# One product over both chunks for the levels of 16 and 32 steps of the first tile

## The chip, the cores and the metric

The program runs on one core of one Trainium2 chip. The metric is the device time of one execution in microseconds (us). Before the change it is 591.69 us, the median of three executions (591.05 to 592.04).

The core's engines work side by side, each through its own list of instructions in order, and wait for one another through semaphores. PE multiplies matrices, and PEld names its loads of weights; DVE, ACT and POOL work on elements; SP starts most DMA transfers. A matmul takes its weights (`lhsT`, a block of rows by columns) and streams the columns of `rhs` past them, and its result goes to PSUM.

## The reference

There are two blocks, one behind the other. The first is a recurrent attention (RWKV-6): for each of 4 batches and 8 heads, over 768 steps of 48 channels, a 48 x 48 state is kept.

```python
for t in range(S):
    cur = einsum('bhd,bhe->bhde', u * k[t], v[t])
    y[t] = einsum('bhd,bhde->bhe', r[t], state + cur)
    state = w[t][..., None] * state + einsum('bhd,bhe->bhde', k[t], v[t])
```

The second takes y, laid out as 3072 tokens of 384 channels, and computes `gelu(x @ w_in) @ w_out` with the exact gelu, 2048 hidden channels and an output of 3072 x 384. `w_in` and `w_out` come as 64-bit numbers and are turned into 32-bit ones on the chip. All matmuls on data are in 32-bit floats.

## The kernel before, in words

**Tiles and units.** The sequence is cut into 8 tiles x = 0 to 7 of T = 384 steps (two for each batch), and a tile into 6 chunks of C = 64 steps. Two heads share the 128 partitions, 64 rows each (48 used), so 8 heads are 4 pairs. Tile 0 alone is worked in two units of two pairs each (`units_of(0)` is 2, so `np_` is 1 there and 2 in later tiles), so that its work can start before all of its data is there. NI = 6 is the number of (pair, double chunk) entries in a unit.

**Inside a chunk.** For step t and an earlier step s of the same chunk, r of t meets k of s through the product of the decays w between them. Tiles 0 and 1 build this 64 x 64 matrix `a_sb` by levels of h = 1, 2, 4, 8, 16 and 32 steps (`halves`). At level h the chunk falls into blocks of 2h steps, and the later half of every block meets its earlier half. A level has three parts:

- `products` (L480): for each entry, each head g and each of its two chunks p, a matmul with the chunk's k as 64 rows x 64 columns of weights and the chunk's r as 64 moving columns. Results of the two chunks go to rows 0 to 63 and 64 to 127 of the PSUM pair `d`, those of the two heads to its two banks. In tile 0 all 64 columns of r are multiplied and the later halves are picked out of the result by a view; later tiles multiply only the 32 columns of the later halves.
- the update (L522, L533): DVE multiplies r and k by decays, in place, for the next level. It can start when the product has read them.
- the copy to `a_sb`: below level 16 by DVE with a mask (L544), at levels 16 and 32 by ACT, one copy (L541) for each block, 4 a unit at level 16 and 2 at level 32.

In tile 0 every `products` call except the one of level 1 ends with `keep_warm(2)` (L253), two matmuls of zeros, 128 x 512 in bf16, whose result nobody reads. The pool of `d` has three pairs of banks, so a product waits for the copies out of the pair used three before.

**After the levels.** PE transposes k (L713, `kt_ps`), ACT copies the result to SBUF (L715, `kx`), PE multiplies k and v of each chunk (L739, `kv_ps`), DVE runs the chain of states over the chunks (L759, L754), and PE multiplies `a_sb` with v (L780) and r with the states (L825) into `y_ps`. ACT and DVE copy y to `xT` (L832, L848), and one pair of heads goes by way of `ysb` (ACT, L851) and six small DMAs (L855, three issued by SP and three by ACT).

**The order of work.** It is written out by hand: each stage is a generator, and the string `PLAN[x]` says whose next step comes. For tile 0, "." and "s" are the two units, "f" the start of tile 1's attention, "c" the conversion of the weights (three ACT passes L361, L362, L364, two DVE passes L373, L377), "l" the loads, "w" the load of tile 1's v, "x" six more matmuls of zeros. Every engine gets its instructions in this order, so the conversions stand between the attention's steps on ACT and DVE. The memsets of L232 and L191 on DVE release loads that SP issues (L233, L192).

**After tile 0.** Tile 1's attention runs beside the projections of tile 0: L1216 makes the hidden rows `h_ps`, ACT applies gelu (L1219, L1221), L1310 and later L1230 multiply with `w_out`. L1004 is the projection in the later tiles.

## Time and profile before

| what | value |
|---|---|
| median of three executions | 591.69 us |
| the profiled execution | 593.44 us, span 591.6 us |
| PE busy, loads of weights busy | 572.6 us (97%), 509.1 us (86%) |
| DVE, ACT busy | 461.9 us (78%), 276.6 us (47%) |
| PE busy from 0 to 10 us | 4.48 us |
| PE busy from 30 to 40 us | 6.39 us |
| PE busy from 50 to 60 us | 10.00 us |
| one product of levels 4 to 32 in tile 0 (L480) | 0.93 us, 48 records of matmuls and 48 of loads |
| a pair of `keep_warm` matmuls there | 0.39 us |
| the 12 copies of levels 16 and 32 (L541) | 4.50 us, from 29.83 us on |
| the first L1216 | at 47.47 us |

The profile shows one execution. A row of the timeline gives the start, the length, engine, line and operation of some instructions of one kind that follow each other, how many (x), and in brackets how long the engine had been idle before them and what ended that. A matmul in 32-bit floats stands in the profile as two records, with two loads of weights. Lengths of single matmuls overlap, so the time of a group is its length as a whole. "Issue" as a cause means that nothing in the profile accounts for the wait.

### The profile page before, as it was taken

To read this page: it belongs to the slowest core of one execution; us is meant where nothing else is said; L and a number is where in the kernel's file an instruction comes from. 1 tells how busy PE (TensorE), PEld (TensorE's weight loads), DVE (VectorE), ACT (ScalarE), POOL (GpSimd) and SP (SyncE) were. 2 spreads that over 40 slices of the span, in tenths; PEclk is the share of its full clock that TensorE was granted. 3 is DMA by queue.
4 is the path that set the end of the run, shared out by engine and by line. 5 is a ranking of instruction groups with operands and counts; after the bars stand their busy time and mean duration, and the time that the engine had idled before them with its cause. 6 is when DMAs were issued, how large, how long until landed. Compare 5 with 4: busy or idle time off the path is not lost. (4 is left out here: it accounts for less than half of the span.)

```text
span 591.6 us, 17427 instructions
## 1 busy us (share of the span) xinstructions
PE 572.6 (97%) x7502; PEld 509.1 (86%) x7516; DVE 461.9 (78%) x905; ACT 276.6 (47%) x640; POOL 8.0 (1%) x21
## 2 busy tenths in 40 slices
PE   6779999999999999999999999999999999999998
PEld 3555666766799999999998999999999999989997
DVE  6969767988969987697859987688768998985532
ACT  2367889323612458045461468235561465523400
POOL 3100000000000000000000000000000000000000
PEclk9999999999999999999999999999999999999999
DMA  6658571020152211241022310420015200210000
GB/s 237 210 173 310 177 268 63 32 91 1 23 147 78 78 51 29 73 134 37 1 56 87 125 37 16 100 88 34 3 26 167 73 2 2 41 39 8 1 14 33
DMA packets 51004, 46.80 MB, mean 79 GB/s; under 512 B 31728, under 2 KB 36080, under 8 KB 50928
## 3 DMA queue, kind: packets, MB, share of 16 engines
q1 hardware_dynamic: 50832, 45.62, 25.6%
q8 instruction: 59, 0.97, 0.7%
q14 instruction: 17, 0.14, 0.1%
q10 hardware_dynamic: 96, 0.07, 0.1%
HBM read 36.24 MB, written 4.72 MB: 69 GB/s over the span
## 5 line engine op out<-in xcount | busy, mean ns | idle before, releaser
L1004 PE MATMUL h_ps<-xT,w_in_sb 128*128 128x192 f32 x408 | 81.2, 330 | 0.1
L1004 PEld LDWEIGHTS h_ps<-xT,w_in_sb 128*128 128x128 f32 x408 | 67.7, 190 | 3.1 <-ACT g L1036 1.2
L1216 PE MATMUL h_ps<-xT,w_in_sb 128*128 128x384 f32 x192 | 64.2, 490 | 0.4 <-DVE tot_sb L439 0.4
L1216 PEld LDWEIGHTS h_ps<-xT,w_in_sb 128*128 128x128 f32 x192 | 35.8, 190 | 24.6 <-ACT kx L429 0.8
L1230 PE MATMUL o_ps<-w_out_sb,g 128*128 128x192 f32 x224 | 39.5, 326 | 0.0
L1230 PEld LDWEIGHTS o_ps<-w_out_sb,g 128*128 128x128 f32 x224 | 37.0, 190 | 0.3
L632 ACT COPY a_sb<-d 32x256 f32<-32x256 f32 (+8 forms) x90 | 32.6, 362 | 4.6 <-PE d L616 3.1
L480 PEld LDWEIGHTS d<-rkw 64*64 64x64 f32 x1152 | 20.1, 142 | 14.1 <-issue 8.4
L1230 PE MATMUL o_ps<-w_out_sb,f 128*128 128x192 f32 x176 | 31.6, 329 | 0.0
L1230 PE MATMUL o_ps<-w_out_sb,e 128*128 128x192 f32 x176 | 31.4, 329 | 0.0
L1230 PE MATMUL o_ps<-t,g 128*128 128x192 f32 x176 | 31.4, 329 | 0.0
L1230 PE MATMUL o_ps<-t,e 128*128 128x192 f32 x176 | 31.2, 328 | 0.0
L1230 PE MATMUL o_ps<-t,s 128*128 128x192 f32 x176 | 30.9, 327 | 0.0
L649 DVE COPY_PREDICATED a_sb<-quarter,d 128x480 f32<-128x480 uint8 (+5 forms) x54 | 23.2, 438 | 8.5 <-PE d L616 7.3
L754 DVE SCALAR_TENSOR_TENSOR st<-st,tot_sb,kv_ps 128x48 f32<-128x48 f32 x160 | 28.9, 258 | 0.9 <-PE kv_ps L739 0.8
L1004 PE MATMUL u_ps<-s,w_in_sb 128*128 128x192 f32 x160 | 29.5, 327 | 0.0
L1230 PEld LDWEIGHTS o_ps<-t,g 128*128 128x128 f32 x176 | 28.7, 190 | 0.4
L1230 PEld LDWEIGHTS o_ps<-w_out_sb,e 128*128 128x128 f32 x176 | 28.7, 190 | 0.3
L1230 PEld LDWEIGHTS o_ps<-w_out_sb,f 128*128 128x128 f32 x176 | 28.7, 190 | 0.3
L1230 PEld LDWEIGHTS o_ps<-t,e 128*128 128x128 f32 x176 | 28.8, 190 | 0.2
L480 PE MATMUL d<-rkw 64*64 64x64 f32 (+1 forms) x1152 | 22.6, 229 | 6.6 <-DMA rkw<-in_rkw_dram 3.2
L1230 PEld LDWEIGHTS o_ps<-t,s 128*128 128x128 f32 x176 | 28.9, 190 | 0.1
(233 smaller groups left out, 1169.6 us busy)
## 6 DMA issues: line engine op xcount, KB each, us to landing
rkw<-in_rkw_dram SPq DMA_DIRECT2D x54, 256.0 KB, 4.1
raw<-in_w_out_dram SPq DMA_DIRECT2D x8, 768.0 KB, 4.6
v_in<-in_v_dram SPq DMA_DIRECT2D x8, 584.0 KB, 4.0
raw<-in_w_in_dram SPq DMA_DIRECT2D x5, 768.0 KB, 6.4
out_dram<-o_sb SPq DMA_DIRECT2D x20, 192.0 KB, 2.1
rkw<-kx SPq DMA_DIRECT2D x72, 48.0 KB, 2.0
rkw<-in_rkw_dram SPq DMA_DIRECT2D x6, 384.0 KB, 4.1
raw<-in_w_in_dram SPq DMA_DIRECT2D x9, 256.0 KB, 4.4
```

The lines of the kernel that those rows point to most:

```text
L480: nc.tensor.matmul(d[half[p], g, n * width:(n + 1) * width], lhsT=kc[half[g], b, i, p], rhs=right(half[g], b, i, p), start=True, stop=True)
L632: nc.scalar.copy(out=at[z, g, first:behind, (a + 1) * h:], in_=d[z, :, :, to] if g == slice(None) else d[z, :, to])
L649: nc.vector.copy_predicated(out=an[:, :, :, :, (a + 1) * h:], mask=mask.to_broadcast(data.shape), data=data)
L754: nc.vector.scalar_tensor_tensor(out=stq[:, q, c], in0=stq[:, q, c - 1] if c else b4[:, q, NC - 1], scalar=totq[:, q, c:c + 1], in1=kvs[q ...
L1004: nc.tensor.matmul(o, lhsT=lhsT, rhs=rhs, start=start, stop=True, skip_group_check=True)
L1216: nc.tensor.matmul(h_ps, lhsT=w_in_sb[:, f // FI, j, f % FI * 128:(f % FI + 1) * 128], rhs=xT[:, j, :], start=(j == 0), stop=(j == NJ - 1))
L1230: nc.tensor.matmul(o, lhsT=lhs(j), rhs=rhs(j), start=start and j == 0, stop=(j == HF - 1), skip_group_check=True)
```

## The change

In tile 0, at the levels 16 and 32, a new function `both_chunks` takes the place of `products`. For each entry and head it makes one matmul: k of both chunks as 64 rows x 128 columns of weights, and the later halves of both chunks' r as 64 moving columns. The result has the two chunks' steps s in its 128 rows, and in its columns first the later halves of chunk 0, then those of chunk 1. Half of it pairs the k of one chunk with the r of the other; that half is never read. A unit's product at these levels has 12 matmuls instead of 24. `keep_warm(2)` follows at level 16 and no longer at level 32. ACT's copies are the same in number and size, and take the columns of their own chunk. The line numbers behind the new function are 13 to 15 higher. Nothing else is edited; the levels below 16 and the other tiles keep their functions.

```diff
+        def both_chunks(h):
+
+            d = pair("d")
+            for n in range(np_ * NI):
+                b, i = divmod(n, NI)
+                for g in range(2):
+                    late_r = rc[half[g], b, i].rearrange("p c (m two j) -> p c m two j", two=2, j=h)[:, :, :, 1, :]
+                    nc.tensor.matmul(d[:, g, n * C:(n + 1) * C], lhsT=kc[half[g], b, i].rearrange("p c t -> p (c t)"),
+                                     rhs=late_r, start=True, stop=True)
+            if not h == LEVELS[-1]:
+                keep_warm(2)
+            return d[:, :, 0:np_ * NI * C].rearrange("p g (n c m j) -> p g n c m j", c=2, j=h, n=np_ * NI)
+
...
             for h in LEVELS:
                 m = C // 2 // h
-                if np_ < NPART:
+                if np_ < NPART and h >= 16:
+                    d = both_chunks(h)
+                elif np_ < NPART:
 
                     d = products(range(np_), lambda z, b, i, p: rc[z, b, i, p], C, h == 1)
...
-                            nc.scalar.copy(out=ah[s, :, :, i], in_=d[s, :, :, i])
+                            nc.scalar.copy(out=ah[s, :, :, i], in_=d[s, :, :, p, i] if np_ < NPART else d[s, :, :, i])
```

## The prediction

> **What bounds the kernel now.** I read the page's shares first, then busy time by stage, then the first tile's stage row by row.

> ```profile
> PE 572.6 (97%) x7502; PEld 509.1 (86%) x7516; DVE 461.9 (78%) x905; ACT 276.6 (47%) x640; POOL 8.0 (1%) x21
> ...
> q8 instruction: 59, 0.97, 0.7%
> ```

> ```profile
> 34.30:47.40 13.10, 8.81 (x373) 7.46 (x374) 8.52 (x32) 7.02 (x12) 0.00 (x0) 1.00 0.41 118
> 47.40:591.60 544.20, 539.11 (x6425) 484.45 (x6426) 426.90 (x798) 255.82 (x606) 0.00 (x0) 1.00 0.23 68
> ```

> In the stage rows the columns after the length are PE, weight loads, DVE, ACT and POOL busy. From 47.4 us on PE is idle for 5 us out of 544: that part is PE's, and moves as one block with the moment at which the first long projection (L1216) starts. In the 13 us before, PE is idle for 4.3 us. So the edit, which ends at 32 us, is worth what it does to that start. ACT and PE there, in order of time (start, length, then what; idle time before it in brackets):

> ```profile
> 27.00 0.94 ACT L361 ACTIVATE f<-raw 128x768 f32<-128x768 f32 x1 [6.09 <-DMA raw<-in_w_in_dram]
> 27.83 1.03 ACT L362 ACTIVATE e<-raw,two 128x768 f32<-128x768 uint32 x1
> 28.89 1.08 ACT L364 ACTIVATE e<-raw 128x768 f16<-128x768 f32 x1
> 29.83 4.50 ACT L541 COPY a_sb<-d 16x192 f32<-16x192 f32 x12
> 34.36 1.50 ACT L715 COPY kx<-kt_ps 128x768 f32<-128x768 f32 x2
> ```

> ```profile
> 31.14 0.93 PE L480 MATMUL d<-rkw 64*64 64x64 f32 x48 [0.24 <-ACT a_sb L541]
> ...
> 32.49 1.80 PE L713 MATMUL kt_ps<-ident,rkw 128*128 128x128 f32 x12
> ```

> ```profile
> 35.21 0.44 PE L739 MATMUL kv_ps<-v_in,kx 64*64 64x48 f32 x14 [0.92 <-ACT kx L715]
> 36.23 0.72 PE L739 MATMUL kv_ps<-v_in,kx 64*64 64x48 f32 x34 [0.58 <-issue]
> 36.74 0.93 PE L780 MATMUL y_ps<-a_sb,v_in 64*64 64x64 f32 x48
> 37.45 0.86 PE L739 MATMUL kv_ps<-v_in,kx 64*64 64x48 f32 x46
> 40.23 0.20 PE L739 MATMUL kv_ps<-v_in,kx 64*64 64x48 f32 x1 [1.92 <-issue]
> ...
> 42.85 1.38 PE L825 MATMUL y_ps<-rkw,st 64*64 64x64 f32 x40 [0.52 <-DVE fence L790]
> ```

> The waits of this stage, summed (who waited for whom: total, times, longest), and below them the longest of PE after 47.4 us:

> ```profile
> DVE st L759 <- PE kv_ps L739: 4.2, 2, 3.0
> ...
> ACT ysb L851 <- PE y_ps L825: 1.8, 1, 1.8
> ```

> ```profile
> PE y_ps L780 <- DVE st L754: 1.1, 3, 0.4
> ```

> Two things are to be seen. From 27.00 to 35.86 ACT works without a pause, started by a weight's DMA and not by PE: the products have slack. Then PE stops twice inside kv_ps, 0.58 and 1.92 us, waiting for nothing ("issue"), and DVE's state chain (L759, L754) and ACT's ysb wait for PE. Those stops look like missing code. The instruction queue moved 0.97 MB in 59 packets, 16 KB each. PE's 15018 instructions are 255 to a packet, 65 bytes each. Between the two stops lie 34+48+46 = 128 matmuls with their loads, 256 instructions. Packets of that queue start at 33.79 and 37.36 us, last 0.95 and 1.36, and PE goes on 1.5 us after each: 37.36+1.36+1.5 = 40.2. Where the DMA is idle a packet starts 1.1 us after PE passes the previous boundary (36.23 to 37.36, 40.23 to 41.35). So the next 256 instructions are there 3.6 to 4.0 us after a boundary, and PE stops if it needs them sooner.

> **The change part by part.**

> *Four products (levels 16 and 32, two units).* Each had 24 matmuls, recorded as 48 loads and 48 matmuls, 0.93 us; it gets 12 with 128 columns of weights, 24 and 24. All four 64x64 squares are busy now: 48 loads in 0.79 us (the last takes 0.13) is one per 14 to 15 ns, 58 ns per square. A 128-column load lasts 190 ns (L1004) where a 64-column one lasts 134 to 142, so it holds its half of the rows some 110 ns; the transposes of L713, 128 columns, 6 in 0.64 us, give 107. Twelve per half, the two halves side by side, plus 0.22 us for the last: 1.5 us. Bounds: 0.55 (24 records at the old spacing) and 2.9 (the halves one after another, 24 x 0.11). I take 1.5, by L713, the nearest row with 128 columns. [...]

> At 1.5 us the products run 26.60-28.10, 28.57-30.07, 30.54-32.04, and 32.0-33.5. ACT wants them at 29.83, 31.11, 32.41 and 33.38: all but the last in time, that one 0.1 late. ACT's chain ends 0.1 later, and kv_ps starts at 35.3 instead of 35.21. As the four follow each other, the delay is 4D + 27.6 - 33.4 for a product of D us: nothing up to 1.45, 1.6 us at D = 1.85, 5.8 at 2.9. Behind them on DVE wait update(k) (L522, 30.63 to 32.09), and in order after it the conversion L377 and the memsets that release three weight DMAs (32.01 to 33.5). Those DMAs are queued behind 768 KB that land at 34.45, so their end moves less: 0.3 us from 37.6, and ACT is free for ysb at 40.9 instead of 40.63, still before it is used (42.37). No other DMA, no SP or POOL instruction is moved past anything.

> *The two warming pairs of level 32.* Four 512-column matmuls, 0.5 us twice with the gap in front. The first lies on the path from the third to the fourth product, and its loss is in the times above; the second would let the transposes start at 32.0, but they wait for ACT's copies (32.4). Worth nothing while ACT leads.

> *Copies L541.* Same partitions, elements and strides of 64 floats: 4.5 us stay.

> *PE's instruction count.* 4 x 48 + 8 = 200 instructions fewer, so every later boundary falls 56 instructions earlier in the code (256 - 200). The stop inside the first kv_ps goes: its boundary now lies at the first transpose. The one 92 instructions into the second kv_ps lies 36 in. Without stops kv_ps and y_ps take 0.73 and 0.71 us, so PE reaches it at 35.3 + 0.73 + 0.71 + 0.27 = 37.0. The fetch for it starts after the boundary at the first transpose (33.4 with D = 1.5, 32.5 with 0.93) plus 1.1, or behind the data queued on its engine: 768 KB until 34.5, then up to three shares of 256 KB, 0.75 each. Available at 37.2 to 38.4: a stop of 0.2 to 1.4 us in place of 0.58 + 1.92. I take 37.7, the middle. The second kv_ps ends 38.4 (was 40.4), its y_ps 39.1 (41.2), the first L825 40.4 (42.3). DVE, busy with the first chain until 38.4, runs the second to 40.7; the second L825 starts at 41.0 (42.85). Its boundary, 20 instructions in, has its code at 37.7 + 1.1 + 1.0 to 1.4 + 1.5 = 41.3 to 41.7, a stop of 0 to 0.4. It ends 42.6 (44.23), the next tile's 96 records and the six warming matmuls (3.2 us as before) at 45.8. ysb starts at 40.9 (42.37), so its DMAs and xT (landed at 47.23) come 1.5 us sooner. The projection starts at 45.8 or 45.9 instead of 47.47.

> *Sum.* -2.5 for the two stops, +0.7 for the new one, +0.1 for ACT, +0.1 to 0.2 at L825: -1.6 us, ends -0.6 and -2.2. After 47.4 us PE waits 1.1 us for L754 and little else; weights come 3 us ahead of use at the tightest (converted at 63.4, used at 66.4), so the block moves whole. The profiled execution took 593.44 (span 591.6), 1.75 above the median 591.69; off its own time 591.8, off the median 590.1.

> **The rivals.**
> - *The new stop is as long as the old ones* (fetch held behind all three weight shares, or xT's DMAs held on the fetch's engine: now one of 16 parts lands 2 us after the rest, at 47.23, behind a code packet of 45.25 to 46.67). For it: the fetch crossed at 29.65 started only at 33.79. Against: data end at 36. Gain 0.5 or so: 591.2.
> - *The halves load one after another* (ends slower). D = 2.9, ACT's chain 5.8 late, less 2.5 for the stops gone: +3.1, 594.8. It decides from D = 1.85. Against it: 48 loads of 134 ns in 0.79 us mean eight in flight in all four squares, so both halves of the rows do load together.
> - *The tensor clock falls.* With two warming pairs gone, PE has only transposes from 32.1 to 35.2. At half clock a product took 1.56 us (at 9.12) against 0.93: 0.63 for each of kv_ps and y_ps, some 3 us until it recovers, +1.2 net: 592.9. Against: 1.9 us of idle before 40.23 did it no harm. [...]
> - *The gain is lost later.* The boundaries move in seven tiles' dense groups too. Now only one stop of under 0.1 us is to be seen there (at 523 us); a group of 192 instructions takes 1.4 us, and a new stop of up to 1 us per unlucky group is possible. 591.7.

> **How the numbers follow.** Forecast 590.1 (589.2 to 590.9): 0.57. Stop as long as before, 591.2: 0.20. Loads in turn, 594.8: 0.10. Clock, 592.9: 0.05. Lost later, 591.7: 0.08. A change of 0.2% is 1.2 us, about what a measurement of this kernel tells from none. Faster by more (under 590.5): nearly all of the first case and a little of the second, 0.56. Within: 0.27. Slower: the two mishaps of PE and a little of the last, 0.17. The range 589.2 to 592.6 leaves out the loads in turn (which hold the bound D = 2.9), most of the clock's case, and a few in a hundred below.

> **What the changed profile would show.** The products: 24 records in 1.2 to 1.6 us each. ACT still unbroken from 27.0 to 36. No "issue" before the first kv_ps's second part; one stop 18 matmuls into the second, 0.2 to 1.4 us. L825 at 39.1 and 41.0, first L1216 at 45.6 to 46.3, every later start earlier by the same. Wrong if the products take over 1.8 us, if the stop in kv_ps ends after 39, if 64-row groups double their time after 35 us, or if L1216 starts 1.6 us sooner and the end does not.

## The result, and the profile after

The change makes the kernel slower: 595.07 us median (592.47 to 599.70, 21 executions) against 591.95 (589.07 to 595.11, 21 executions) for the kernel before, a ratio of 1.0063 with a 95% interval of 1.0044 to 1.0083. The forecast was 590.1, and its range ended at 592.6.

The 21 executions of the changed kernel fall in two groups by the mean clock granted to PE: in 8 it is 0.983 to 0.989 and they take 596.7 to 599.7 us (median 598.85), in 13 it is 0.994 to 1.000 and they take 592.5 to 595.3 (median 593.96). In what follows these are called the low-clock and the full-clock executions. So there are two losses: one of 2.0 us in the median of the 13, and one of about 5 us more that strikes in 8 of 21. The profile of the changed kernel is a full-clock one, 593.51 us, span 591.7. First its page:

```profile
PE 575.9 (97%) x7416; PEld 511.4 (86%) x7416; DVE 461.5 (78%) x905; ACT 276.9 (47%) x640; POOL 8.0 (1%) x21
...
q8 instruction: 58, 0.95, 0.7%
```

One code packet fewer, as the 200 instructions should give, and yet PE is busy 3.3 us longer. ACT in order of time, in the columns of the prediction:

```profile
29.80 2.55 ACT L556 COPY a_sb<-d 16x192 f32<-16x192 f32 x8
32.66 0.95 ACT L556 COPY a_sb<-d 32x384 f32<-32x384 f32 x2 [0.31 <-PE d L495]
34.00 0.95 ACT L556 COPY a_sb<-d 32x384 f32<-32x384 f32 x2 [0.39 <-PE d L495]
34.98 1.50 ACT L730 COPY kx<-kt_ps 128x768 f32<-128x768 f32 x2
40.37 0.91 ACT L361 ACTIVATE f<-raw 128x768 f32<-128x768 f32 x1 [3.90 <-DMA raw<-in_w_in_dram]
```

The copies start at 29.80 as before, ACT waits 0.7 us for products, and then, which is new, 3.9 us for the raw weights (before, it started that pass at 37.75). PE over the same stretch:

```profile
27.01 1.55 PE L495 MATMUL d<-rkw 64*128 64x64 f32 x24 [0.51 <-DVE rkw L548]
...
31.06 2.90 PE L495 MATMUL d<-rkw 64*128 64x64 f32 x48
...
35.83 0.92 PE L754 MATMUL kv_ps<-v_in,kx 64*64 64x48 f32 x48 [0.26 <-ACT kx L730]
...
37.28 0.50 PE L754 MATMUL kv_ps<-v_in,kx 64*64 64x48 f32 x18
40.05 0.99 PE L754 MATMUL kv_ps<-v_in,kx 64*64 64x48 f32 x28 [2.28 <-issue]
...
47.76 1.04 PE L253 MATMUL warm<-zeros 128*128 128x512 bf16 x4 [0.74 <-issue]
48.63 1.78 PE L1231 MATMUL h_ps<-xT,w_in_sb 128*128 128x384 f32 x5
```

The products take 1.55 us. The stop in the first kv_ps is gone, and the one 18 matmuls into the second is where it was forecast, but 2.28 us long, and there is another in the six warming matmuls of tile 1. From the first kv_ps to the first long projection it takes 12.8 us, 12.26 before; 45.8 us was forecast for the projection and 48.63 came. The weight DMAs as SP issues them, and the busy share of the DMA engines from 30 to 40 us, in slices of a quarter of a microsecond (tenths), each first before and then after the change:

```profile
32.11 1.29 SPq L233 DMA_DIRECT2D raw<-in_w_in_dram  x3
```

```profile
34.14 1.29 SPq L233 DMA_DIRECT2D raw<-in_w_in_dram  x3
```

```profile
DMA  4949887999999989999999741000030000000000
```

```profile
DMA  5199179989999998510083689998998200000000
```

They are issued 2.0 us later than before (34.14 against 32.11). The transfer in front of them ends at 34.3, the DMA engines stand nearly idle for 0.7 us, and the new data fills them from 35.0 to 37.8. The code packet that the second kv_ps needs starts at 37.72, lasts 0.93 and PE goes on 1.4 us after it. The last 16 KB of the weights, 8 packets of 2 KB, move only behind that packet, from 38.64 to 39.8, and ACT's pass, which waits for them, starts at 40.37.

The low-clock executions look otherwise. This is one, the changed kernel profiled again (596.29 us); first PE, then stretches of it with PE, loads, DVE, ACT and POOL busy, the granted clock, and the DMA's share and rate:

```profile
28.74 2.83 PE L495 MATMUL d<-rkw 64*128 64x64 f32 x24
...
32.47 5.39 PE L495 MATMUL d<-rkw 64*128 64x64 f32 x48
37.79 2.80 PE L728 MATMUL kt_ps<-ident,rkw 128*128 128x128 f32 x12
40.52 0.92 PE L754 MATMUL kv_ps<-v_in,kx 64*64 64x48 f32 x48
```

```profile
27.00:30.40 3.40, 3.40 (x26) 2.45 (x26) 1.16 (x3) 2.74 (x6) 0.00 (x0) 0.50 0.50 107
30.40:34.00 3.60, 3.60 (x28) 2.65 (x28) 0.96 (x1) 1.24 (x4) 0.00 (x0) 0.50 0.77 281
34.00:37.00 3.00, 3.00 (x32) 3.00 (x32) 1.45 (x5) 0.94 (x2) 0.00 (x0) 0.50 0.03 5
```

The clock is at half (0.50) from 26.79 to 40.44, four windows of 3.41 us, though the records show PE busy without a pause. One such window takes 0.003 off the mean clock of an execution (half of 3.41 us in 592), so a mean below 0.990 stands for four or more; the 0.986 here is these four and one at 9.7 us. At half a product takes 2.83 us, the fourth ends at 37.8 instead of 33.9, and kv_ps starts at 40.5 instead of 35.8.

### The profile page after: what moved, and what is told of

Its sections match the earlier page's. It is cut to its first block, busy times and chain, and to the rows that moved or that the text cites. A ratio compares the mean times of both kernels' runs of the same rounds, so it can differ in the third digit from the quotient of the medians.

```text
span 591.7 us, 17241 instructions
## 1 busy us (share of the span) xinstructions
PE 575.9 (97%) x7416; PEld 511.4 (86%) x7416; DVE 461.5 (78%) x905; ACT 276.9 (47%) x640; POOL 8.0 (1%) x21
## 4 chain that ended last, share of the span: by engine, by line
PE 90%; DVE 6%; issue 2%; DMA 1%; ACT 0%; SPq 0%; DVEq 0%
PE o_ps L1245 30%; PE h_ps L1019 15%; PE u_ps L1019 12%; PE h_ps L1231 11%; PE d L631 4%; PE o_ps L1325 4%; PE d L480 3%; PE y_ps L795 2%; PE y_ps L840 2%; PE kv_ps L754 2%; PE c_ps L1019 2%; DVE st L769 2%; DMA rkw<-in_rkw_dram 1%; PE d L495 1%; PE warm L253 1%
## 5 line engine op out<-in xcount | busy, mean ns | idle before, releaser
L1231 PEld LDWEIGHTS h_ps<-xT,w_in_sb 128*128 128x128 f32 x192 | 35.8, 190 | 24.0 <-ACT xT L847 0.2
L647 ACT COPY a_sb<-d 32x256 f32<-32x256 f32 (+8 forms) x90 | 32.6, 363 | 4.6 <-PE d L631 3.1
L631 PE MATMUL d<-kx,rkw 64*64 64x96 f32 x1056 | 28.2, 248 | 0.0
L631 PEld LDWEIGHTS d<-kx,rkw 64*64 64x64 f32 x1056 | 23.1, 133 | 5.8 <-issue 5.0
```

The source lines that it names most:

```text
L631: nc.tensor.matmul(o[half[p], i * 3 * C // 2:(i + 1) * 3 * C // 2], lhsT=kc[half[g], n // NI, n % NI, p], rhs=rx[half[g], 2 * n + p], star ...
L647: nc.scalar.copy(out=at[z, g, first:behind, (a + 1) * h:], in_=d[z, :, :, to] if g == slice(None) else d[z, :, to])
L1231: nc.tensor.matmul(h_ps, lhsT=w_in_sb[:, f // FI, j, f % FI * 128:(f % FI + 1) * 128], rhs=xT[:, j, :], start=(j == 0), stop=(j == NJ - 1))
```

## The experiments

The medians are of all executions of a kernel; "before" is the kernel before on the same chip, run beside it.

**e1, the changed kernel again.**

> The changed kernel once more, for its spread and for the clock of each run. In its first profile the products took 1.55 us, PE stood 2.28 us inside the second kv_ps until 40.05 (code packet from 37.72), the tensor clock halved from 39.8 to 43.2 us, and L1216 began at 48.63 instead of 47.47. Theory A (late start: longer products put the weight DMAs and the code behind them later): about +1.2 us in every run, ratio 1.002, the clock unimportant. Theory B (the clock): the runs fall in two groups, those with a mean clock of 0.99 or more at +1 to +2 us, those with 0.983 to 0.989 at +5 to +8 us, and the ratio stays at 1.004 to 1.008.

596.55 us (592.2 to 598.84, 6 executions), before 591.44 (29): ratio 1.0081 [1.0050, 1.0112]. Three of six are low-clock (0.982 to 0.986: 596.3, 598.7, 598.8). None of the 29 of the kernel before is below 0.991. The low clock belongs to the kernel, not to one chip: e6 and e12, each on another chip, have it too.

**e2, the two warming pairs of level 32 put back.**

```diff
-            if not h == LEVELS[-1]:
-                keep_warm(2)
+            keep_warm(2)
```

> The changed kernel with keep_warm(2) behind level 32 again (two pairs, 8 PE instructions more). Theory B, where the missing pairs let the clock fall: mean clock 1.000 or 0.997 in every run, no run 5 us above the others, ratio 1.000 to 1.003. Theory A: the third and fourth product move apart by another 0.5 us, ACT's copies and the weight DMAs with them, ratio 1.004 to 1.008, L1216 at 48.5 to 49.2. If the pause inside kv_ps is what lets the clock fall, the pairs 8 us earlier don't help, and the low clocks stay.

593.04 us (590.29 to 600.73, 12), before 591.44. Four of 12 are low-clock, 598.6 to 600.7, and in the profile of one the clock is at half from 27.26 to 44.32, five windows. So the missing warming pairs are not why the clock stays down. The 8 full-clock ones have a median of 592.3, 0.8 above the kernel before where the changed kernel has 2.0; eight executions are too few to say whether the pairs gain something.

**e3, the changed kernel with 100 small matmuls in front** (one column each, 200 instructions, as many as the change took away), so that code boundaries stand where they stood before.

```diff
     keep_warm(8)
+    pad_ps = ps.tile([128, BANK], F32, name="pad_ps", tag="mm", bufs=2)
+    for _ in range(100):
+        nc.tensor.matmul(pad_ps[0:32, 0:1], lhsT=zeros[:, 0:32], rhs=zeros[:, 0:1], start=True, stop=True)
```

> The changed kernel with 100 matmuls of 32 x 1 behind the first warming (200 PE instructions, in PE's idle time from 5.9 to 9.1 us), so that from the levels 16 and 32 on the boundaries of 256 instructions lie in the code where they lay before the change. Theory C (the place of the code boundaries is the loss): the stops in kv_ps are those of before, one 29 instructions into the first, one 92 into the second, ratio within 0.999 to 1.002. Theory A (the products' length): L1216 still about 1 us late and the ratio 1.002 or more, as the weight DMAs are still released at 34 us instead of 32.

593.2 us (591.05 to 598.41, 12), before 591.44: ratio 1.0042 [1.0023, 1.0062]. Two of 12 are low-clock. In the profile the second kv_ps stops 1.22 us near its end, where the kernel before stops, the warming matmuls do not stop, and from the first kv_ps to the first long projection it is 10.7 us instead of 12.8. The stops are where theory C put them, but the ratio is not within its range; e13 shows a reason.

**e4, the kernel before with 28 of them in front** (56 instructions): the boundaries of the changed kernel in the kernel before.

> The kernel before with 28 matmuls of 32 x 1 behind the first warming (56 PE instructions), so that the code boundaries from level 16 on lie where the changed kernel has them (the second kv_ps is cut 37 instructions in), with the products and warming pairs of before. Theory C: a stop of about 2 us in the middle of the second kv_ps, L1216 about as late as in the changed kernel, and its low clocks: ratio 1.002 to 1.006. Theory A: the code arrives in time or nearly (packet at 34 to 36 us, stop under 1.2 us), L1216 at 46 to 47, ratio 0.996 to 0.999.

592.95 us (590.29 to 595.34, 12), before 591.44: ratio 1.0021 [1.0002, 1.0039]; no execution below 0.994. The profile has the changed kernel's two stops, 1.58 us 18 matmuls into the second kv_ps and 0.74 in the warming matmuls. It also has a fall of the clock, at 25.13, and this one is over after a single window. So the moved boundaries alone bring the stops and not the low-clock group.

**e5, the kernel before once more.**

> The kernel before, unedited, for a second profile and the clock of each run. Its first profile was of an execution 1.75 us above the median. Theory: the two stops in kv_ps (2.5 us) that the forecast counted as gained are in that length an accident of that execution; here the code packets come sooner, the stops last 0.5 to 1.5 us together, L1216 begins at 46.3 to 46.9, ratio 0.999 to 1.001, no mean clock under 0.990. Rival: the stops are the same 2.5 us and L1216 is at 47.3 to 47.6.

591.45 us, before 591.59 (29): no difference. The use of it is the profile (589.84 us):

```profile
38.21 0.20 PE L739 MATMUL kv_ps<-v_in,kx 64*64 64x48 f32 x1 [1.32 <-issue]
...
45.17 2.17 PE L1216 MATMUL h_ps<-xT,w_in_sb 128*128 128x384 f32 x6
```

One stop of 1.32 us where the first profile had 0.58 and 1.92, and 10.6 us from kv_ps to the projection instead of 12.26. The 2.5 us of stops that the forecast meant to remove were partly an accident of one execution.

**e6, five warming matmuls behind each new product** (`keep_warm(5)` at both levels).

> The changed kernel with keep_warm(5) behind each of its four products (in place of 2 at level 16 and 0 at level 32). Theory D (the clock monitor goes by streamed columns; the new products stream for 107 of 226 ns of each load at half clock, so a clock that has fallen before them stays down until kv_ps): more streaming between them lifts the clock within one or two windows of 3.4 us, so no run under 0.990, and the spread of 6 us goes; ratio 1.001 to 1.004. Rival (something else in the new products holds the clock, their form of 64 rows by 128 columns): a third of the runs stays at 0.982 to 0.989 and 598 us or more.

596.46 us (594.52 to 601.56, 6), before 591.59: ratio 1.0100 [1.0061, 1.0138]. Two of six are at 0.989 and 0.991 (600.2, 601.6); the profile of the first has the clock at half for three windows, 26.6 to 36.84. More warming did not keep the fall away, which lasts three windows there, and the other four took 594.5 to 597.1.

**e7, the kernel before with its 64x64 products streaming only 32 columns** at levels 16 and 32, as later tiles do: same loads, same number of instructions, same warming, half the streamed columns.

```diff
-                if np_ < NPART:
+                if np_ < NPART and h < 16:
```

> The kernel before, with the products of levels 16 and 32 in tile 0 streaming only the 32 columns of the later halves (as the later tiles do): the same instructions, loads of 64 columns and warming pairs, half the streamed columns. Products 0.90 to 0.93 us. Theory D: loads of 58 ns with 27 ns of streaming, the same share as in the changed kernel, so runs under 0.990 appear here too (one in five or more), ratio 1.001 to 1.006. Rival (the 128-column form or the longer products matter, not the streamed columns): no such runs, ratio 0.998 to 1.001.

592.2 us (589.64 to 597.16, 12), before 591.59. Nine executions are like the kernel before (median 591.1). Three are at 0.991, 0.991 and 0.986, with 594.4, 595.6 and 597.2 us; none of the 29 of the kernel before beside it was below 0.993. The profile of the last, PE:

```profile
26.68 1.00 PE L480 MATMUL d<-rkw 64*64 64x64 f32 x25 [2.31 <-issue]
...
28.73 1.50 PE L480 MATMUL d<-rkw 64*64 64x32 f32 x48 [0.51 <-DVE rkw L533]
```

The clock is at half from 26.58 to 40.23, the same four windows as in the changed kernel, without any 128-column load. PE has pauses in them (2.89 of 3.40 us busy from 27.0 to 30.4). By the count of low clocks alone e7 does not stand out from e8 and e13, which stream all 64 columns (table below), so it rests on this one profile.

**e8, the kernel before with 64 small matmuls in front** (128 instructions).

> The kernel before with 64 matmuls of 32 x 1 behind the first warming (128 PE instructions), so that code boundaries lie 60 instructions into the first y_ps and 28 into the first L825 instead of inside the two kv_ps. If the place of the boundaries sets the stops: none in kv_ps, one of up to 1.5 us in the first L825, L1216 0.5 to 1.2 us sooner than in the kernel before, ratio 0.998 to 0.999. If the stops are short anyway in most executions: ratio 0.9995 to 1.001.

593.17 us (590.75 to 596.65, 12), before 591.59: ratio 1.0032 [1.0010, 1.0054]. No stop in kv_ps, one of 1.26 us in tile 1's first product. One execution is at 0.989 (596.7 us) and one at 0.991.

**e9, the new products streaming all 128 columns of r.** The later halves come first, then the halves that nobody reads, which the next product's results overwrite. Loads and instructions stay.

```diff
-            for n in range(np_ * NI):
+            for n in reversed(range(np_ * NI)):
...
-                    late_r = rc[half[g], b, i].rearrange("p c (m two j) -> p c m two j", two=2, j=h)[:, :, :, 1, :]
-                    nc.tensor.matmul(d[:, g, n * C:(n + 1) * C], lhsT=kc[half[g], b, i].rearrange("p c t -> p (c t)"),
-                                     rhs=late_r, start=True, stop=True)
+                    both_r = rc[half[g], b, i].rearrange("p c t -> p (c t)").rearrange("p (q two j) -> p two q j", two=2, j=h)
+                    nc.tensor.matmul(d[:, g, n * C:(n + 2) * C], lhsT=kc[half[g], b, i].rearrange("p c t -> p (c t)"),
+                                     rhs=both_r, start=True, stop=True)
```

> The changed kernel, but each product with 128 columns of weights now streams all 128 columns of r of both chunks (later halves first, then the halves that nobody reads, which the next product's results overwrite). Same loads, same number of instructions, twice the columns streamed. Theory S (what keeps the clock at half is that the new products stream too few columns for their loads: 64 per load of 128): executions with a mean clock below 0.990 go from 8 in 21 to at most 1 in 12, a fall at 27 us is over after one window of 3.4 us, and the median is that of the changed kernel's undisturbed executions, 593 to 594 us. Rival L (the length of the products, or the 128-column load itself, keeps the clock down): a third of the executions stay at 0.982 to 0.989 and 597 to 600 us. In both the product takes 1.5 to 1.6 us at the full clock.

594.0 us (592.6 to 595.7, 12), before 591.52 (35): ratio 1.0030 [1.0008, 1.0051]. No execution is below 0.994. The profile:

```profile
26.03 1.61 PE L495 MATMUL d<-rkw 64*128 64x128 f32 x24 [0.83 <-DVE rkw L548]
...
39.26 0.62 PE L754 MATMUL kv_ps<-v_in,kx 64*64 64x48 f32 x28 [2.31 <-issue]
...
47.56 1.04 PE L253 MATMUL warm<-zeros 128*128 128x512 bf16 x4 [1.48 <-issue]
48.43 2.10 PE L1231 MATMUL h_ps<-xT,w_in_sb 128*128 128x384 f32 x6
```

Twice the columns take 0.06 us longer a product (1.61 for 1.55), so the streamed columns hardly set its time. With them the low-clock group is gone, and the loss of the full-clock executions stands as it was, with its two stops. The length of the products and the width of the loads, which are those of the changed kernel, do not hold the clock down. No profile with 128 streamed columns (e9, e14, e17, e18) has a fall at this place, so whether the clock comes back at once or does not fall is not seen.

**e10 and e11, the new product at one level alone**, at the other the 64x64 products with their warming pairs.

```diff
-                if np_ < NPART and h >= 16:
+                if np_ < NPART and h == 16:
```

> The new product at level 16 alone; level 32 has its two 64x64 products and its warming pairs as before. Theory S: the level-16 products lie at 26.6 to 31 us, in the windows in which the clock falls, so a sixth to a third of the executions are below 0.990, with a fall of two or three windows instead of four; undisturbed ones 592.5 to 593.5, since the memsets behind the update (and with them the weight DMAs) are released about 1 us late. Rival W (the missing warming pairs of level 32 are the cause): no execution below 0.990, 591.5 to 592.5 us.

> The new product at level 32 alone, without the two warming pairs behind it; level 16 as before. Theory S: a fall at 27 us is over before these products start at 30.5 us, or takes one more window; at most 1 execution in 12 below 0.990, 591.5 to 592.5 us, the memsets not later than in the kernel before. Rival W (the missing warming pairs are the cause): a third of the executions below 0.990, 597 us or more.

Level 16 alone: 592.35 us (590.32 to 598.25, 12), before 591.52, with three of 12 at 0.988 to 0.991 (595.0, 595.9, 598.3) and three windows at half in the profile (28.52 to 38.76). Level 32 alone: 590.92 us (589.65 to 593.25, 12), nothing below 0.994. The level-16 products lie where the clock falls; those of level 32 come behind it. Nor do the missing warming pairs of level 32 matter here.

**e12, the changed kernel with the memsets earlier**: in the written order of tile 0, the second conversion pass on DVE and the three memsets that release the weight DMAs stand ahead of the second unit's last update.

```diff
-    0: ".lls.....sslsc.lsslll.sl.sls..sl.lscsl..sss.lscs.lscs.s.clll.s..s.cccsss...wss..ss.ff",
+    0: ".lls.....sslsc.lsslll.sl.sls..sl.lscsl..sss.lscs.lscsclll.s..s..s.cccsss...wss..ss.ff",
```

> The changed kernel with tile 0's written order changed in one place, so that the second conversion pass on DVE and the three memsets that release the weight DMAs stand ahead of the second unit's last update instead of behind it. Theory A (in executions at the full clock the change loses 1 to 2 us because the longer products hold up the update, and with it the memsets, the weight DMAs, the code packet queued behind them and the next conversion): the weight DMAs are issued at 31.0 to 32.5 us instead of 34.1, ACT's wait for the raw weights at 40.4 shrinks from 3.9 to under 2.5 us, the first long projection starts about 1 us earlier and the executions at the full clock have a median of 592 to 593 instead of 593 to 594. Rival (the loss comes from the stop for code, wherever the weight DMAs stand): no earlier than the changed kernel. In both a third of the executions still fall below 0.990.

593.14 us (591.47 to 598.26, 12), before 591.52. Five of 12 are low-clock, and its profile is one of them, so the forecast starts of the weight DMAs are read in e14. The 7 full-clock ones have a median of 592.7, 1.2 above the kernel before where the changed kernel's were 2.0 above; so few do not tell the two apart.

After these twelve the low clock had its cause, the columns that the new products stream. Open was what the full-clock executions lose: late weight DMAs, or the moved code boundaries.

**e13, the kernel before with 128 small matmuls in front**, exactly one packet of code, so that the boundaries do not move.

> The kernel before with 128 small matmuls (one column each) put in front: 256 instructions, exactly one code packet, so that every boundary stands at the same instruction as in the kernel before. Theory B (28 and 64 of these matmuls made the kernel 1.5 us slower because they moved the boundaries): no difference from the kernel before, 591 to 592 us. Rival P (the small matmuls, or one packet more to fetch, cost it themselves): 593 us or more.

594.71 us (593.63 to 597.0, 12), before 591.17 (35): ratio 1.0058 [1.0036, 1.0080]; three of 12 are at 0.988 to 0.991. The small matmuls cost something themselves: the first kv_ps starts at 37.47, where the kernel before has 35.21 and 34.59. The profile shows one place, a stop in the second product; that PE comes to the end of its loaded code sooner is the likely reason, not a shown one.

```profile
13.41 0.58 PE L484 MATMUL d<-kx,rkw 64*64 64x64 f32 x9 [1.47 <-issue]
```

So the medians of e3, e4 and e8 can't be read as the price of a moved boundary; their profiles can, since they show where the stops stand. From the first kv_ps on, e13 has the stops of the kernel before (one, 1.44 us, none in the warming matmuls) and takes 10.6 us to the projection, as e5 does.

**e14, e9 and e12 together**: 128 streamed columns and the earlier memsets.

> The 128 streamed columns (no fall of the clock) together with the second conversion pass and the three memsets ahead of the second unit's last update. Theory A (late weight DMAs are what executions at the full clock lose): 592.5 us or less, weight DMAs issued at 31 to 32.5 instead of 33.3 us, first long projection by 47.5 us. Rival B (the boundaries, which stand where they stood without the edit of the order): 593.5 to 594.5 us. In both no execution below a mean clock of 0.990.

592.89 us (590.78 to 594.46, 12), before 591.17: ratio 1.0018 [0.9998, 1.0038]; nothing below 0.994. The weight DMAs, the DMA engines from 30 to 40 us, and PE:

```profile
30.14 1.40 SPq L233 DMA_DIRECT2D raw<-in_w_in_dram  x3
```

```profile
DMA  5974998999989999899999981000000000000200
```

```profile
38.13 0.62 PE L754 MATMUL kv_ps<-v_in,kx 64*64 64x48 f32 x28 [0.63 <-issue]
...
46.16 1.04 PE L253 MATMUL warm<-zeros 128*128 128x512 bf16 x4 [1.17 <-issue]
47.03 2.10 PE L1231 MATMUL h_ps<-xT,w_in_sb 128*128 128x384 f32 x6
```

The gap between the transfers is closed. Against the changed kernel the data ends at 36.0 instead of 37.8, the code packet starts at 35.8 instead of 37.72 (an estimate: 2.33 us ahead of 38.13, where PE goes on, as in the changed kernel), and the stop in kv_ps is 0.63 instead of 2.28 us; the projection starts 1.4 us earlier than in e9. The stop in the warming matmuls stays. The median misses the 592.5 of that theory by 0.4, and the interval of the ratio just reaches 1.

**e15, e11 with the earlier memsets, and e16, e11 again.**

> The new product at level 32 alone, with the memsets ahead of the second unit's last update. Theory A: weight DMAs at 31 to 32 instead of 32.6 us, 590.0 to 590.9 us, up to 1 us faster than without the edit of the order. Rival B (the weight DMAs are not what the start of the projection waits for here): 590.9 us as without it, or more, because the second unit's update comes later. No execution below 0.990 in either.

> The new product at level 32 alone once more, for its verdict against the kernel before on another chip. If it is the gain of one warming pair and fewer loads: 590.5 to 591.2, 0.5 us below the kernel before. If the first measurement was chance: no difference.

591.34 us (590.48 to 592.2, 12) and 591.10 (590.08 to 594.06, 12), before 591.17: ratios 0.9997 [0.9978, 1.0016] and 0.9992 [0.9973, 1.0012]. Level 32 alone is no measurable gain, and the order does nothing for it. The profile of e16 has a fall of the clock, at 26.96, that is over at 30.38, while the level-16 products stream 64 columns for 64:

```profile
27.00:30.40 3.40, 3.40 (x83) 2.18 (x72) 1.89 (x6) 3.33 (x7) 0.00 (x0) 0.50 0.46 106
30.40:34.00 3.60, 3.60 (x54) 3.17 (x53) 2.44 (x7) 2.49 (x8) 0.00 (x0) 1.00 0.80 282
```

**e17, e14 with the 100 small matmuls of e3 in front, and e18, e14 again**, on one chip: all three causes mended, and two of them.

> 128 streamed columns, the memsets ahead of the second unit's last update, and 100 small matmuls in front (200 instructions, as many as the change took away), so that the code boundaries stand where they stood before. If the moved boundary is the rest of the loss: no stop for code in the six warming matmuls, 10.5 to 10.8 us from the first kv_ps to the first long projection (11.5 in e14), and about 1 us faster than e18, 591.0 to 592.2, level with the kernel before; from this the small matmuls may take up to 0.5 us at the start. Rival (the rest is the longer products alone, PE's work that nothing hides): no faster than e18. No execution below a mean clock of 0.990 in either.

> The kernel of e14 again, beside e17 on one chip: 592.5 to 593.2 us, 1.2 to 1.8 over the kernel before, with a stop of about 1 us in the six warming matmuls in its profile.

e17: 591.37 us (590.35 to 592.76, 12), before 591.58 (23): ratio 0.9997 [0.9986, 1.0007]. e18: 592.03 (590.04 to 594.77, 12), ratio 1.0011 [0.9992, 1.0030], less than was expected of it. None of the 24 is below 0.990. PE in e17:

```profile
38.94 0.20 PE L758 MATMUL kv_ps<-v_in,kx 64*64 64x48 f32 x1 [1.10 <-issue]
...
44.44 1.47 PE L253 MATMUL warm<-zeros 128*128 128x512 bf16 x5
45.75 2.10 PE L1235 MATMUL h_ps<-xT,w_in_sb 128*128 128x384 f32 x6
```

No stop in the warming matmuls (1.51 us in e18), and 10.2 us from kv_ps to the projection against 11.55 in e18. With all three mended, the loss is gone, and no gain is left. The small matmuls hide none that the profile shows: the first kv_ps starts at 35.53, in e18 at 35.60. The boundary's own price is not settled by the times. The two medians are 0.7 us apart, too little to tell them apart with executions of e18 that spread over 4.7 us, and the one kernel of e14 and e18 was 1.7 above the kernel before on one chip and 0.5 on the other. What shows the boundary is the profile, by 1.3 us.

What the executions with a mean clock below 0.990 say together:

| products of levels 16 and 32 in tile 0 | kernels | below 0.990 |
|---|---|---|
| 128-column loads, 64 columns streamed | changed kernel, e1, e2, e3, e6, e12 | 23 of 69 (one more at 0.991) |
| the same at level 16 alone | e10 | 1 of 12 (two more at 0.991) |
| the same at level 32 alone | e11, e15, e16 | 0 of 36 |
| 128-column loads, 128 columns streamed | e9, e14, e17, e18 | 0 of 48 (one at 0.991) |
| 64-column loads, 32 columns streamed | e7 | 1 of 12 (two more at 0.991) |
| 64-column loads, 64 columns streamed | kernel before, beside the experiments | 0 of 151 (four at 0.991) |
| the same, with small matmuls in front | e4, e8, e13 | 2 of 36 (three more at 0.991) |

Where the clock was low in the executions of the last row no profile shows.

## Why the prediction was wrong

The median came 5.0 us above the forecast: 0.3 because the kernel before stood higher this time (591.95 for 591.69), 3.6 because the full-clock executions lost 2.0 where 1.6 were to be gained, and 1.1 by the low clock. The steps that failed are the terms for PE's code (-2.5 for two stops, +0.7 for a new one, nothing behind it), the 0.3 us for the weight DMAs, and the reason for which the clock was to fall.

**Products, 1.5 us: right** at the full clock (1.55), from the row of the transposes. That the two halves of the rows load side by side was right too, so the rival of loads in turn falls (1.55, not 2.9).

**ACT's copies and chain: nearly right.** 4.5 us of copies, 0.7 us of waits for products; the first kv_ps 8.8 us after the start of the first product, 8.6 before.

**The warming pairs, worth nothing: not contradicted.** e11 lacks them at level 32 and loses nothing; e2 leaves it open. (The 0.39 us given for a pair before is one matmul's; where both are recorded, in the changed kernel, a pair takes 0.60.)

**The clock's rival, 0.05 at 592.9: the danger was seen, the reason was wrong.** It looked for the danger in a gap, the 3.1 us of transposes behind the products, and had PE recover after some 3 us. In the low-clock profiles of kernels with the new level-16 product (e1, e2, e6, e10, e12) the clock went down at 26.6 to 28.5, about where the first of these products runs, and stayed down through the products themselves, for three to five windows. (The changed kernel's own profile has a fall of one window, at 39.8, behind the stop in kv_ps; from there to the projection it took 8.58 us, and e9, without a fall, 9.17.) What had to be asked was not whether PE pauses but what the products do for a clock that has just fallen. Streaming as many columns as are loaded, it was back after one window (e4, e16); streaming half as many, it was not (e1, e7, e10). In e9 nothing but the streamed columns and the order of the products was changed, and the group was gone. It is not columns for each microsecond that count: in e1 the clock came back behind the window from 37.03 to 40.44, most of which the transposes fill, and these stream 12 x 128 columns in 2.80 us where a product streams 24 x 64 in 2.83. But the transposes stream as many columns as they load. In all six low-clock profiles (these and e7) the clock came back behind the first window more than half of which went to other work than the products that stream half. So the transposes seem to count: in e1 that window has nothing else but the last 0.8 us of a product. (That the clock was at half at 9.12 the profile before does not show, since its record of the clock starts at 15.06. The changed kernel's does: there the same product, at 9.19, takes 1.56 us at a granted 0.50, in a fall from 9.11 to 12.53.) In the median of 21 executions this is the 1.1 us between 593.96 and 595.07; in each low-clock execution it is 5.

Nor did a busy PE by itself bring the clock back: by the records PE was busy 10 of 10 us from 27.0 to 37.0 in e1, and the granted clock stayed at 0.50.

**The count of PE's code: the boundaries right, the stops wrong, three times.** The boundary 18 matmuls into the second kv_ps was there.
- *-2.5 us for two stops that go.* They were read off one execution. In e5 the same kernel stops once, for 1.32, and takes 10.6 us from the first kv_ps to the projection. The forecast's own 10.5 (35.3 to 45.8) is no better, so there was next to nothing to gain.
- *+0.7 for the new stop.* It took 2.28. The packet was reckoned from "data end at 36", and the data ended at 37.8.
- *The boundary behind it was not followed to the projection.* The forecast went as far as L825 and then took "3.2 us as before" for tile 1's product and warming. 256 instructions behind the boundary in the second L825 comes the next one, in the warming matmuls, and PE stops there for 0.74 to 1.5 us (changed kernel, e4, e9, e14, e18). Where the boundaries stand as before it lies in the slow matmuls of the projection and costs nothing to be seen (e3, e5, e13, e17).

**The weight DMAs, "0.3 us": wrong.** The delay of the memsets was nearly right (34.04, 33.5 forecast). But they are behind 768 KB only as long as these last. That transfer was over at 34.3, and the late ones, issued from 34.14 on, ran from 35.0, so their lateness came through nearly whole: data end at 37.8 against 36.0 where they are early (e14), the code packet with it, and ACT's conversion, behind the last 16 KB, at 40.37 instead of 37.75. On ACT it did no harm, since ysb (44.07, 42.37 before) waited 0.80 us for PE and not for ACT; it told through the code packet. In the profile of e14, where the memsets are early, the stop is 0.63 us.

**The projection block moves whole: right within 1 us.** From the first long projection to the end it is 543.07 us here and 544.13 before, and 542.7 to 545.1 over all full-clock profiles. But the prediction had two results, 591.8 off the profiled execution's own time and 590.1 off the median, and took the second. The stretch from kv_ps to the projection was 1.7 us longer in that execution than in e5, about the 1.75 us by which it lay above the median: the stops to be gained were read in an unusually long execution, and the gain was taken off an ordinary one.

The sum: full-clock executions +2.0 instead of -1.6, of which the missing gain at the two stops, the longer new stop and the one in the warming matmuls make up most (12.8 us from the first kv_ps to the projection, 10.6 in e5); then +1.1 in the median for the clock. That the late weight DMAs and the moved boundaries together are the 2 us is shown by e17, which has neither and is level with the kernel before. How they share it is not settled.

## What to carry to other kernels

Where twice the streamed columns cost a product next to nothing (1.61 us for 128 columns, 1.55 for 64), fewer save nothing and can keep the clock down once it has fallen (three to five windows of 3.41 us here), at 1.8 times the price (2.83 us); ask of each dense stretch what it streams, not only whether PE pauses. An edit that changes the number of instructions moves the code boundaries behind it (200 fewer here, or 56 more in e4, put the stop in the second kv_ps behind 18 of its matmuls instead of 46), so follow each boundary to the first slow stretch, and don't count a stop as a gain before a second execution shows it. A DMA that is queued behind another is covered only until that one ends (34.3 us here, and the late ones ran from 35.0): put the two ends side by side before calling a late release free.
